# The last output block in row halves: the fifth product's share added by GpSimd, the first half's sum added to the last PSUM bank by TensorE, and that bank turned by VectorE straight from PSUM

## The chip, the cores and the metric

The kernel runs on one core of a Trainium2 chip. A core has five engines with a queue each: TensorE (PE, matmuls; PEld is its weight loads), VectorE (DVE), ScalarE (ACT), GpSimd (POOL) and SyncE (SP, which only issues transfers here). Each queue is worked off in order; engines wait for each other by semaphores. ScalarE issues some of the output transfers beside its own work. The metric is the device time of one execution in microseconds (us); lower is better.

## The reference

Pooled attention, then a feed-forward block with a snake activation:

```python
k_p = k.reshape(B, H, Sp, 8, D).mean(axis=3)        # B=8, H=8, S=576, D=64
v_p = v.reshape(B, H, Sp, 8, D).mean(axis=3)
attn = softmax(q @ k_p.T / sqrt(D)) @ v_p
x = attn.transpose(0, 2, 1, 3).reshape(4608, 512)
h = x @ w_in                                        # 512 -> 2048
g = h + sin(alpha * h) ** 2 / alpha
out = g @ w_out                                     # 2048 -> 512, float32
```

The change lies in the last matrix product, `g @ w_out`, and there in its last block alone.

## The kernel before

The first two thirds of the time are attention and `x @ w_in`; `g` goes through a buffer in HBM. The function `outputs` then computes `g @ w_out`, in eight units u of 576 rows (`self.B` units), by a two-level scheme of fast matrix multiplication with seven products instead of eight at each level. The outer seven products p run in the order `ORDER = (1, 2, 4, 6, 7, 5, 3)`; the loop over k takes the 56 pairs (u, n) one after the other, and a 57th pass finishes the last of them.

An outer product consists of seven inner products, `product(st, q, out, start)` (L1337), each a sum over `NJ` = 4 matmuls of 128x128 weights with 144 columns in fp32; the trace shows each such matmul as two records, eight for one inner product. The results are gathered in three PSUM banks: `x0` and `x1` with two parts of 144 columns each, and `yz`. The bank `x0` belongs to the first 144 rows of the half unit (i = 0), `x1` to the next 144 (i = 1). In both, part h = 0 and part h = 1 are two groups of 128 output columns. `yz[:, 1]`, the result of the fifth inner product, is a term z that both h = 1 parts still need. Pass k does products 1, 6 and 7 of its own outer product and, between them, 5, 4, 2 and 3 of the one before (functions `fifth`, `fourth`, `second`, `third`). ScalarE copies partial results from bank to bank (L1443, L1468, L1488).

When an outer product is complete, `combine` (L1370) adds its parts to block accumulators in SBUF, `c["a"]`, `c["b"]`, `c["c"]` (tiles `ca`, `cb`, `cc` of [128, 2, 2, 144], index h, then i). A finished block is turned in 32x32 squares by VectorE (`out`, L1357; L1362 is the transpose) into a tile `o`, and stored by four transfers (L1367). In the last unit the transfers alternate between the queues of SyncE and ScalarE (`both`).

The order of all instructions is the order in which the Python code emits them, engine by engine (`tc.manual_schedule`). Only the waits are put in by the framework.

The end of the kernel, with what the change touches:

- Pass 55 (p = 3 of the last unit starts): `combine` of p = 5 copies its banks to `cb`, adds z to it, lets GpSimd add all of `cb` to `cc` (L1390), lets VectorE add it to `ca`, and puts `ca`'s output on the list `later`, which runs at the end of this pass: one transpose and four transfers, two of them on ScalarE's queue.
- Pass 56, TensorE: products 5, 4, 2, 3 of the last p = 3, and nothing else.
- Pass 56, VectorE: after product 4, `early` (L1346) adds z to both h = 1 parts of `cc` and `x1` to its i = 1 half, and turns and stores the block's columns of rows 160 to 287 (`n0 = 5`: four groups of 32). After products 2 and 3, `combine` adds `x0` to the i = 0 half (L1412) and turns and stores rows 0 to 159.

Of the kernel before, what the change touches and what calls it, by code (L numbers as in the profile page):

```python
# [13 lines left out]
F32 = mybir.dt.float32  # L14
AX = mybir.AxisListType.X
AF = mybir.ActivationFunctionType
OP = mybir.AluOpType
PSUM = bass.MemoryType.PSUM

P = 128  # L20
# [20 lines left out]
class Kernel:  # L41
# [1248 lines left out]
    def outputs(self):  # L1290

        nc, T = self.nc, self.T
# [3 lines left out]
        add = lambda o, a, b: tt(o, a, b, OP.add)  # L1296
        X, C = {}, {}
        self.ne = False

        def outer(u, n):  # L1300
            r = self.R
            if n == 0:
                X[u] = {1: r["r11"], 2: r["r12"], 4: r["r22"]}
                return
            new = lambda p: self.gs.tile([P, self.NJ, JW, 2, T], F32, name=f"x{p}")[:]
            x = X[u]
            if n == 1:
                x[5] = new(5)
                tt(flat(x[5]), flat(r["r21"]), flat(x[4]), OP.add)
            if n == 2:  # L1310
                x[6] = new(6)
                tt(flat(x[6]), flat(x[5]), flat(x[1]), OP.subtract)
            if n == 3:
                x[7] = r["r21"]
                tt(flat(x[7]), flat(x[1]), flat(x[7]), OP.subtract)
            if n == 4:
                x[3] = new(3)
                tt(flat(x[3]), flat(x[2]), flat(x[6]), OP.subtract)
# [15 lines left out]
            yield  # L1334
            tt(s4, a(1, 2), s2, OP.subtract)

        def product(st, q, out, start):  # L1337
            A, W = st["A"][q], self.W[st["p"]][q]
            for J in range(self.NJ):
                nc.tensor.matmul(out, W[:, J // 2, J % 2, :], A[:, J, :], start=(start and J == 0), stop=(J == self.NJ - 1), skip_group_check=True)  # L1340

        def block(n):

            return self.op.tile([P, 2, 2, T], F32, name=n)

        def early(st):  # L1346

            t = C[st["u"]]["c"]
            with_z(t, st["yz"])
            add(t[:, :, 1], t[:, :, 1], st["x1"][:])  # L1350
            if st["u"] == self.B - 1:
                out(st["u"], 0, 1, t, 5, queues=both)

        def with_z(t, z):
            add(t[:, 1], t[:, 1], z[:, 1:2, :].to_broadcast([P, 2, T]))

        def out(u, i, j, t, n0=0, n1=2 * T // 32, queues=4 * (nc.sync,)):  # L1357

            if n0 or n1 * 32 == 2 * T:
                C[u]["o"] = self.op.tile([P, 2 * T // 32, 2, 32], F32, name="o", bufs=3)  # L1360
            o = C[u]["o"]
            nc.vector.transpose(out=o[:, n0:n1].rearrange("p n h c -> p h n c"),  # L1362
                                in_=t[:].rearrange("p h i c -> p h (i c)").rearrange("p h (n c) -> p h n c", c=32)[:, :, n0:n1])
            r = u * self.S + i * 2 * T
            for a in range(4):
                c = j * 2 * P + a * 64
                queues[a].dma_start(out=self.out[r + 32 * n0:r + 32 * n1, c:c + 64].rearrange("(n k) c -> k n c", k=32),  # L1367
                                        in_=o[32 * a:32 * a + 32, n0:n1].rearrange("k n h c -> k n (h c)"))

        def combine(st):  # L1370

            u, p, x, z = st["u"], st["p"], (st["x0"], st["x1"]), st["yz"]
            c = C.setdefault(u, {})

            def with_x(o, t):
                for i in range(2):
                    add(o[:, :, i], t[:, :, i], x[i][:])
            if p in (1, 4, 5):

                n = "a" if p == 1 else "b"  # L1380
                t = c[n] = block("c" + n)
                for i in range(2):
                    nc.scalar.copy(out=t[:, :, i], in_=x[i][:])
                with_z(t, z)
                if p == 5 and u < self.B - 1:
                    add(c["a"][:], c["a"][:], t[:])
                    out(u, 1, 1, c["a"])
                    add(c["c"][:], c["c"][:], t[:])
                elif p == 5:
                    nc.gpsimd.tensor_tensor(out=c["c"][:], in0=c["c"][:], in1=t[:], op=OP.add)  # L1390
                    add(c["a"][:], c["a"][:], t[:])
                    later.append(lambda: out(u, 1, 1, c["a"], queues=both))
            elif p == 2:
                o = block("cd")
                with_x(o, c["a"])
                with_z(o, z)
                out(u, 0, 0, o)
            elif p == 6:

                t = c["c"] = block("cc")  # L1400
                with_x(t, c["a"])
                with_z(t, z)
            elif p == 7:

                t = c["a"]
                with_x(t, c["c"])
                with_z(t, z)
                add(c["b"][:], c["b"][:], t[:])
                out(u, 1, 0, c["b"])
            else:  # L1410
                t = c["c"]
                add(t[:, :, 0], t[:, :, 0], x[0][:])  # L1412
                if u < self.B - 1:
                    out(u, 0, 1, t)
                else:
                    out(u, 0, 1, t, 0, 5, both)

        both = 2 * (nc.sync, nc.scalar)
        later = []
        last = None  # L1420
# [6 lines left out]
        for k in range(len(seq) + 1):  # L1427
            st = None
            if k < len(seq):
                u, n = seq[k]  # L1430
                st = {"u": u, "p": ORDER[n], "A": A.pop((u, n))}
                if 0 < n < 5 and k != 1:
                    outer(u, n)
                if n == 3 and u + 1 < self.B:
                    self.load_g(u + 1, ("r11", "r12", "r22"))
                if n == 5 and u + 1 < self.B:
                    self.load_g(u + 1, ("r21",))
                if n == 6 and u + 1 < self.B:
                    outer(u + 1, 0)
                x0 = st["x0"] = self.bank([P, 2, T])  # L1440
                yz = st["yz"] = self.abank([P, 2, T])
                product(st, 1, yz[:, 0, :], True)
                nc.scalar.copy(out=x0[:], in_=yz[:, 0:1, :].to_broadcast([P, 2, T]))  # L1443
                if k == 0:
                    yield
            def fifth():
                product(last, 5, last["yz"][:, 1, :], False)

            def fourth():
                product(last, 4, last["x1"][:, 0, :], False)  # L1450
                if last["p"] == 3:
                    early(last)

            def second():
                product(last, 2, last["x0"][:, 0, :], False)

            def third():
                product(last, 3, last["x0"][:, 1, :], False)

            if last:  # L1460
                fifth()
                if k == 1:
                    second()
                fourth()
            if st:
                product(st, 6, x0[:, 1, :], False)
                x1 = st["x1"] = self.bank([P, 2, T])
                nc.scalar.copy(out=x1[:, 0, :], in_=x0[:, 1, :])  # L1468
                if k + 1 < len(seq):
                    sums = inner(*seq[k + 1])  # L1470
                    next(sums)
                    if k == 0:
                        yield
                    next(sums)
            if last:
                if k != 1:
                    second()
                third()
                if k == 5:
                    self.inner_w(3, self.gs)  # L1480
                combine(last)
            for _ in sums:
                pass
            if k == 1:
                outer(0, 1)
            if st:
                product(st, 7, x1[:, 0, :], False)
                nc.scalar.copy(out=x1[:, 1, :], in_=x1[:, 0, :])  # L1488
            if later:
                later.pop()()  # L1490
            last = st
# [117 lines left out]
```

## Time and profile before

| | us |
|---|---|
| median of the runs (902.67, 902.79, 903.61) | 902.79 |
| the profiled execution, device time | 902.87 |
| its span, first to last instruction | 901.0 |
| TensorE busy (7010 matmul records) | 894.6 |
| VectorE busy | 678.0 |
| ScalarE busy | 447.9 |
| GpSimd busy | 212.5 |

Busy time overlaps between engines. The span begins with the first instruction; the device time has 1.87 us around it. Times in the text that look like 894.62 are microseconds from the span's start. A line such as `894.62 1.14 PE L1340 MATMUL ... x8` in the timeline gives start, duration of the whole group, engine, source line, operation, tiles (written<-read), shape and number; a matmul's record has 286 ns, but the next one starts 122.5 ns after it, since they are pipelined.

### The profile page before, as it was taken

To read this page: it belongs to the slowest core of one execution; us is meant where nothing else is said; L and a number is where in the kernel's file an instruction comes from. 1 tells how busy PE (TensorE), PEld (TensorE's weight loads), DVE (VectorE), ACT (ScalarE), POOL (GpSimd) and SP (SyncE) were. 2 spreads that over 40 slices of the span, in tenths; PEclk is the share of its full clock that TensorE was granted. 3 is DMA by queue.
4 is the path that set the end of the run, shared out by engine and by line. 5 is a ranking of instruction groups with operands and counts; after the bars stand their busy time and mean duration, and the time that the engine had idled before them with its cause. 6 is when DMAs were issued, how large, how long until landed. Compare 5 with 4: busy or idle time off the path is not lost.

```text
span 901.0 us, 17940 instructions
## 1 busy us (share of the span) xinstructions
PE 894.6 (99%) x7010; PEld 816.3 (91%) x7010; DVE 678.0 (75%) x1010; ACT 447.9 (50%) x1071; POOL 212.5 (24%) x218
## 2 busy tenths in 40 slices
PE   9999999999999999999999999999999999999998
PEld 5787888888888888888888999999999999999997
DVE  7776867768576675764558799979798888889895
ACT  5687776877768777687976611211111111111111
POOL 5698443825337262430000000000000000000000
PEclk9999999999999999999999999999999999999999
DMA  9957957759586585557226346261618172534401
GB/s 264 245 153 206 243 146 210 189 164 253 139 222 184 180 222 145 171 158 282 94 82 223 101 146 191 66 191 35 224 30 230 31 201 64 172 92 127 138 15 40
DMA packets 128371, 141.13 MB, mean 157 GB/s; under 512 B 46416, under 2 KB 95328, under 8 KB 128288
## 3 DMA queue, kind: packets, MB, share of 16 engines
q1 hardware_dynamic: 125504, 137.88, 53.4%
q10 hardware_dynamic: 2784, 2.11, 0.9%
q8 instruction: 56, 0.92, 0.5%
q14 instruction: 27, 0.22, 0.1%
HBM read 75.37 MB, written 47.19 MB: 136 GB/s over the span
## 4 chain that ended last, share of the span: by engine, by line
PE 97%; DVE 2%; DMA 1%; SPq 0%; issue 0%; ACT 0%; DVEq 0%
PE PS L848 46%; PE PS L1340 41%; PE PS L1038 3%; PE PS L317 2%; PE PS L612 2%; PE PS L625 1%; DMA h<-in_v_dram 1%; DVE x L1295 1%; DVE s L1295 0%; DVE r L1295 0%; PE PS L568 0%; PE PS L570 0%; PE PS L289 0%; PE PS L278 0%; PE PS L478 0%; SPq L164 0%
## 5 line engine op out<-in xcount | busy, mean ns | idle before, releaser
L848 PE MATMUL PS<-home,a 128*128 128x256 f32 x1104 | 258.1, 381 | 0.1
L848 PEld LDWEIGHTS PS<-home,a 128*128 128x128 f32 x1104 | 205.3, 190 | 32.3 <-issue 4.6
L848 PE MATMUL PS<-home,as 128*128 128x256 f32 x768 | 182.6, 381 | 0.0
L848 PEld LDWEIGHTS PS<-home,as 128*128 128x128 f32 x768 | 141.8, 190 | 19.7 <-ACT PS L822 1.2
L1390 POOL TENSOR_TENSOR cc<-cc,cb 128x576 f32<-128x576 f32 x1 | 2.0, 1977 | 501.7 <-DVE cb L1295 501.7
L1340 PE MATMUL PS<-s,wb 128*128 128x144 f32 x896 | 119.1, 286 | 0.0
L1340 PEld LDWEIGHTS PS<-s,wb 128*128 128x128 f32 x896 | 113.7, 190 | 0.1
L1015 ACT ACTIVATE s<-s,c 128x256 f32<-128x256 f32 (+1 forms) x228 | 113.5, 565 | 0.0
L821 DVE TENSOR_TENSOR h<-PS,p 128x512 f32<-128x512 f32 x72 | 49.3, 684 | 64.0 <-PE PS L848 37.4
L131 POOL TENSOR_TENSOR kvin<-kvin 96x768 f32<-96x768 f32 (+3 forms) x42 | 73.8, 1756 | 70.3 <-DMA kvin<-in_v_dram 68.1
L1468 ACT COPY PS<-PS 128x144 f32<-128x144 f32 x56 | 14.7, 263 | 145.0 <-PE PS L1340 138.4
L1008 ACT ACTIVATE s<-h,al 128x256 f32<-128x256 f32 x144 | 65.6, 509 | 38.3 <-DVE h L821 38.3
L1340 PE MATMUL PS<-r,wb 128*128 128x144 f32 x512 | 73.3, 286 | 0.3 <-DVE r L1295 0.3
L1340 PE MATMUL PS<-s,a 128*128 128x144 f32 x512 | 73.2, 286 | 0.0
L1008 ACT ACTIVATE s<-PS,al 128x256 f32<-128x256 f32 x144 | 60.2, 471 | 18.8 <-PE PS L848 17.9
L1060 DVE TENSOR_TENSOR h<-PS,s 128x512 f32<-128x512 f32 x36 | 24.8, 689 | 57.4 <-ACT s L1015 57.4
L1340 PEld LDWEIGHTS PS<-r,wb 128*128 128x128 f32 x512 | 67.1, 190 | 0.5 <-DVE r L1295 0.5
L1340 PEld LDWEIGHTS PS<-s,a 128*128 128x128 f32 x512 | 67.1, 190 | 0.0
L822 ACT COPY PS<-PS 128x512 f32<-128x512 f32 x72 | 41.5, 576 | 35.4 <-PE PS L848 30.6
L1488 ACT COPY PS<-PS 128x144 f32<-128x144 f32 x56 | 14.7, 263 | 88.1 <-PE PS L1340 88.1
L1340 PE MATMUL PS<-x,wb 128*128 128x144 f32 x384 | 54.9, 286 | 0.0
L1340 PE MATMUL PS<-s,we 128*128 128x144 f32 x384 | 54.9, 286 | 0.0
(216 smaller groups left out, 1407.5 us busy)
## 6 DMA issues: line engine op xcount, KB each, us to landing
g_bridge<-h SPq DMA_DIRECT2D x72, 512.0 KB
r<-g_bridge SPq DMA_DIRECT2D x31, 1152.0 KB
out_dram<-o SPq DMA_DIRECT2D x122, 72.0 KB
kvin<-in_k_dram SPq DMA_DIRECT2D x14, 576.0 KB
q<-in_q_dram SPq DMA_DIRECT2D x7, 1024.0 KB
kvin<-in_v_dram SPq DMA_DIRECT2D x14, 512.0 KB
aM<-tr SPq DMA_DIRECT2D x54, 92.0 KB
aM<-tr SPq DMA_DIRECT2D x54, 88.0 KB
```

What stands on the lines that cost most here:

```text
L131: self.nc.gpsimd.tensor_tensor(out=t[..., 0:w] if w > D else out, in0=t[..., 0:w], in1=t[..., w:2 * w], op=OP.add)
L317: nc.tensor.matmul(ps[e][r0 + r:r0 + r + q.shape[-1], h, :], q[s], kb[s, hp, :], start=True, stop=True)
L612: nc.tensor.matmul(o[r:r + 64], w, x, start=start and i < 2, stop=False, skip_group_check=True)
L821: add = lambda o, x, y: nc.vector.tensor_tensor(out=o, in0=x, in1=y, op=OP.add)
L822: copy = lambda o, x: nc.scalar.copy(out=o, in_=x)
L848: nc.tensor.matmul(ps[:, jj, :], self.A[p][:, kk, f * P:(f + 1) * P], x[:, kk, :], start=(start and n == 0), stop=(kk == 1), skip_group_ch ...
L1008: self.nc.scalar.activation(out=G.s[:, i, jj, j, :], in_=src[:, jj], func=AF.Sin, scale=self.al[:, f:f + 1])
L1015: self.nc.scalar.activation(out=x, in_=x, func=AF.Square, scale=self.c[:, f:f + 1])
L1038: nc.tensor.matmul(o, W[m][:, G.J - J0], X[m], start=start and n == 0, stop=True, skip_group_check=True)
L1060: add = lambda o, x, y: self.nc.vector.tensor_tensor(out=o, in0=x, in1=y, op=OP.add)
L1340: nc.tensor.matmul(out, W[:, J // 2, J % 2, :], A[:, J, :], start=(start and J == 0), stop=(J == self.NJ - 1), skip_group_check=True)
L1468: nc.scalar.copy(out=x1[:, 0, :], in_=x0[:, 1, :])
```

## The change

The last block (`cc` of unit 7 at p = 3) is handled in another way; all other blocks keep their instructions and order.

- GpSimd's one add of `cb` to `cc` becomes two, one for each row half i; the second of them is emitted in pass 56 (list `more`).
- z is no longer added by VectorE. ScalarE copies it from PSUM to a new tile `zc` (128x144), and GpSimd adds it to the h = 1 part of each half.
- `early` then adds `x1` to the i = 1 half as before. New: ScalarE copies 16 columns of that half (rows 144 to 159, h = 1) into the `x0` bank, behind its 288 columns, so that the bank holds rows 0 to 159 of h = 1 in one piece.
- In the third product, ahead of its last matmul, TensorE adds `cc[:, 1, 0]` to the bank by a matmul with the identity matrix.
- At the end VectorE adds `x0` only to the h = 0 part (128x144 instead of 128x288), turns 160 columns of that part from SBUF and 160 columns of the h = 1 part from the PSUM bank; the four transfers are as before.
- `out` is split into `turned` (the transpose) and `stored` (the transfers).

```diff
@@ -1334,9 +1334,11 @@
             yield
             tt(s4, a(1, 2), s2, OP.subtract)

-        def product(st, q, out, start):
+        def product(st, q, out, start, plus=None):
             A, W = st["A"][q], self.W[st["p"]][q]
             for J in range(self.NJ):
+                if plus is not None and J == self.NJ - 1:
+                    nc.tensor.matmul(out, self.ident[:], plus, start=False, stop=False, skip_group_check=True)
                 nc.tensor.matmul(out, W[:, J // 2, J % 2, :], A[:, J, :], start=(start and J == 0), stop=(J == self.NJ - 1), skip_group_check=True)

         def block(n):
@@ -1345,27 +1347,42 @@

         def early(st):

-            t = C[st["u"]]["c"]
-            with_z(t, st["yz"])
+            t, z = C[st["u"]]["c"], st["yz"]
+            if st["u"] < self.B - 1:
+                with_z(t, z)
+                add(t[:, :, 1], t[:, :, 1], st["x1"][:])
+                return
             add(t[:, :, 1], t[:, :, 1], st["x1"][:])
-            if st["u"] == self.B - 1:
-                out(st["u"], 0, 1, t, 5, queues=both)
+            nc.scalar.copy(out=self.PS[:, st["bank"]][:, 2 * T:2 * T + 16], in_=t[:, 1, 1, 0:16])
+            o = C[st["u"]]["o"] = self.op.tile([P, 2 * T // 32, 2, 32], F32, name="o", bufs=3)
+            turned(o, row(t), 5, 9)
+            stored(st["u"], 0, 1, o, 5, 9, both)

         def with_z(t, z):
             add(t[:, 1], t[:, 1], z[:, 1:2, :].to_broadcast([P, 2, T]))

-        def out(u, i, j, t, n0=0, n1=2 * T // 32, queues=4 * (nc.sync,)):
-
-            if n0 or n1 * 32 == 2 * T:
-                C[u]["o"] = self.op.tile([P, 2 * T // 32, 2, 32], F32, name="o", bufs=3)
-            o = C[u]["o"]
-            nc.vector.transpose(out=o[:, n0:n1].rearrange("p n h c -> p h n c"),
-                                in_=t[:].rearrange("p h i c -> p h (i c)").rearrange("p h (n c) -> p h n c", c=32)[:, :, n0:n1])
+        def row(t):
+
+            return t[:].rearrange("p h i c -> p h (i c)")
+
+        def turned(o, t, n0, n1, h0=0, h1=2):
+
+            nc.vector.transpose(out=o[:, n0:n1, h0:h1].rearrange("p n h c -> p h n c"),
+                                in_=t[:, h0:h1, 32 * n0:32 * n1].rearrange("p h (n c) -> p h n c", c=32))
+
+        def stored(u, i, j, o, n0, n1, queues=4 * (nc.sync,)):
+
             r = u * self.S + i * 2 * T
             for a in range(4):
                 c = j * 2 * P + a * 64
                 queues[a].dma_start(out=self.out[r + 32 * n0:r + 32 * n1, c:c + 64].rearrange("(n k) c -> k n c", k=32),
                                         in_=o[32 * a:32 * a + 32, n0:n1].rearrange("k n h c -> k n (h c)"))
+
+        def out(u, i, j, t, queues=4 * (nc.sync,)):
+
+            o = self.op.tile([P, 2 * T // 32, 2, 32], F32, name="o", bufs=3)
+            turned(o, row(t), 0, 9)
+            stored(u, i, j, o, 0, 9, queues)

         def combine(st):

@@ -1387,7 +1404,9 @@
                     out(u, 1, 1, c["a"])
                     add(c["c"][:], c["c"][:], t[:])
                 elif p == 5:
-                    nc.gpsimd.tensor_tensor(out=c["c"][:], in0=c["c"][:], in1=t[:], op=OP.add)
+                    for i in (1, 0):
+                        more.append((c["c"][:, :, i], t[:, :, i]))
+                    plus(*more[0])
                     add(c["a"][:], c["a"][:], t[:])
                     later.append(lambda: out(u, 1, 1, c["a"], queues=both))
             elif p == 2:
@@ -1409,12 +1428,21 @@
                 out(u, 1, 0, c["b"])
             else:
                 t = c["c"]
-                add(t[:, :, 0], t[:, :, 0], x[0][:])
                 if u < self.B - 1:
+                    add(t[:, :, 0], t[:, :, 0], x[0][:])
                     out(u, 0, 1, t)
-                else:
-                    out(u, 0, 1, t, 0, 5, both)
-
+                    return
+                o = c["o"]
+                add(t[:, 0, 0], t[:, 0, 0], x[0][:, 0])
+                turned(o, row(t), 0, 5, 0, 1)
+                nc.vector.transpose(out=o[:, 0:5, 1], in_=self.PS[:, st["bank"]][:, T:T + 160].rearrange("p (n c) -> p n c", c=32))
+                stored(u, 0, 1, o, 0, 5, both)
+
+        def plus(o, x):
+
+            nc.gpsimd.tensor_tensor(out=o, in0=o, in1=x, op=OP.add)
+
+        more = []
         both = 2 * (nc.sync, nc.scalar)
         later = []
         last = None
@@ -1438,6 +1466,7 @@
                 if n == 6 and u + 1 < self.B:
                     outer(u + 1, 0)
                 x0 = st["x0"] = self.bank([P, 2, T])
+                st["bank"] = self.turn
                 yz = st["yz"] = self.abank([P, 2, T])
                 product(st, 1, yz[:, 0, :], True)
                 nc.scalar.copy(out=x0[:], in_=yz[:, 0:1, :].to_broadcast([P, 2, T]))
@@ -1449,13 +1478,20 @@
             def fourth():
                 product(last, 4, last["x1"][:, 0, :], False)
                 if last["p"] == 3:
+                    if last["u"] == self.B - 1:
+                        t, zc = C[last["u"]]["c"], self.op.tile([P, T], F32, name="zc", bufs=1)
+                        nc.scalar.copy(out=zc[:], in_=last["yz"][:, 1, :])
+                        plus(t[:, 1, 1], zc[:])
+                        plus(*more[1])
+                        plus(t[:, 1, 0], zc[:])
                     early(last)

             def second():
                 product(last, 2, last["x0"][:, 0, :], False)

             def third():
-                product(last, 3, last["x0"][:, 1, :], False)
+                at_end = last["u"] == self.B - 1 and last["p"] == 3
+                product(last, 3, last["x0"][:, 1, :], False, C[last["u"]]["c"][:, 1, 0] if at_end else None)

             if last:
                 fifth()
```

## The prediction

> **What bounds the kernel now.** I read the chain that ended last first, because the edit touches only the last block of the last unit. Its shares over the whole span:
>
> ```profile
> PE 97%; DVE 2%; DMA 1%; SPq 0%; issue 0%; ACT 0%; DVEq 0%
> ```
>
> TensorE sets the time; VectorE and the transfers count only where TensorE has run out. The same chain for the stretch from 880 us:
>
> ```profile
> 879.96 16.80 PE PS L1340 x137
> 896.75 0.02 issue
> 896.77 0.47 DVE cc L1295
> 897.24 0.02 issue
> 897.26 0.51 DVE o L1362
> ```
>
> So the end is: TensorE without a gap to 896.74 us, one VectorE add, one transpose to 897.77, then the last output transfer and the closing of the program, 3.27 us up to 901.04. The last stretch, engine by engine, from the timeline (start, duration, what; the bracket is idle time and who ended it):
>
> ```profile
> 893.14 1.98 POOL L1390 TENSOR_TENSOR cc<-cc,cb 128x576 f32<-128x576 f32 x1 [501.68 <-DVE cb L1295]
> 893.63 1.14 PE L1340 MATMUL PS<-x,we 128*128 128x144 f32 x8
> 893.89 0.78 DVE L1362 STREAM_TRANSPOSE o<-ca 128x576 f32<-128x576 f32 x1
> ...
> 894.62 1.14 PE L1340 MATMUL PS<-x,wb 128*128 128x144 f32 x8
> ...
> 894.70 3.97 ACTq L1367 DMA_DIRECT2D out_dram<-o  x6
> 895.15 1.04 DVE L1295 TENSOR_TENSOR cc<-cc,PS 128x288 f32<-128x288 f32 x2 [0.49 <-POOL cc L1390]
> ...
> 895.60 1.14 PE L1340 MATMUL PS<-s,wb 128*128 128x144 f32 x8
> 896.23 0.45 DVE L1362 STREAM_TRANSPOSE o<-cc 128x256 f32<-128x256 f32 x1
> 896.77 0.46 DVE L1295 TENSOR_TENSOR cc<-cc,PS 128x288 f32<-128x288 f32 x1
> 897.26 0.51 DVE L1362 STREAM_TRANSPOSE o<-cc 128x320 f32<-128x320 f32 x1
> ```
>
> To be seen: the fourth product (from 893.63), the second (from 894.62) and the third (from 895.60) follow each other at 122.5 ns a matmul; nothing holds TensorE. GpSimd's one add ends at 895.12, VectorE waits 0.49 us for it, and that wait is covered by TensorE, which runs to 896.74. ScalarE's queue holds the six output issues behind VectorE's transposes; the first two are the store of `ca`:
>
> ```profile
> 894.70 0.89 ACTq L1367 DMA_DIRECT2D out_dram<-o  x2
> 895.12 0.47 ACTq L1367 DMA_DIRECT2D out_dram<-o  x1
> ```
>
> They wait for the transpose that ends at 894.67 and keep the queue until 895.59. That matters after the change: ScalarE starts no later instruction while it issues. Elsewhere in this trace:
>
> ```profile
> 66.65 2.81 ACTq L523 DMA_DIRECT2D aM<-tr  x4
> 69.51 0.91 ACT L1008 ACTIVATE s<-h,al 128x256 f32<-128x256 f32 x2 [3.81 <-DVE h L821]
> ```
>
> The activation begins 0.05 us after the fourth issue ends (66.65 + 2.81 = 69.46); the engine stood idle during all four.
>
> **The change, part by part.** Up to `ca`'s transpose (894.67) and its two issues (895.59), every engine has the same instructions in the same order, so these times stay. From there the built program has a new chain through five engines. Its waits: `zc` stands on ScalarE behind the two issues of `ca`; GpSimd's second add waits for `zc`; VectorE's early add (`cc[:, :, 1] += x1`) for that add; ScalarE's 16-column copy into the last bank for the early add; and the first matmul of the *second product* for that copy, although it writes columns 0 to 143 of the bank and the copy columns 288 to 303 (same bank, earlier in program order). Before, the second product waited for nothing. Queued behind it on TensorE is all that is left: second product, third product, identity matmul; VectorE's last add waits for their end, and the last transfers for VectorE.
>
> Step by step, with durations from rows:
>
> - `zc`, 128x144 from PSUM: 895.59 + 0.05 = 895.64. The 128x128 copy from PSUM at L384 has 271 ns, the 128x288 one at L1383 402: 0.28, end 895.92. Bounds: at 514.92 an issue of 0.39 us let the next activation start 0.25 us after its beginning, so 0.14 to 0.18 us earlier; not later.
> - GpSimd, 128x144 add of `zc`: its first add (the `i=1` half of t) starts at 893.14 as before. GpSimd adds of 64, 128 and 256 columns take 321, 457 and 727 ns (L131), about 0.19 us + 2.1 ns a column. For 288 that is 0.80, plus at most the 0.58 us by which the 128x576 add exceeded this line (1.98 against 1.40): end by 894.52, hidden under ScalarE's issues. The `zc` add starts 0.08 us after its releaser (893.06 to 893.14), 896.00, and takes 0.49: end 896.49. The upper bound is the 946 ns of the slow 128x128 row at L806, +0.46; VectorE waits during this add, so I take the undisturbed rows.
> - VectorE's early add, 128x288 with PSUM: 0.03 + 0.455: 896.52 to 896.98.
> - ScalarE's copy of 128x16, SBUF to PSUM: no such row. Below is the 128x1 copy at L619 (160 ns), above the 128x64 one at L392 (213); 0.18. With 0.03 for the release, end 897.19.
> - TensorE: a released weight load starts 0.05 us after its releaser (535.78 to 535.83), 897.24 instead of 894.62: **a stall of 2.62 us**. In that same row the second matmul came 0.227 us after the first, not 0.122: +0.11. Then 16 matmuls as before and two more for the identity (one fp32 matmul is two records): +0.245. Last end 896.74 + 2.62 + 0.11 + 0.245 = 899.71.
> - Identity matmul's own wait: GpSimd goes on from 896.49 with 0.07 + 0.80 and 0.07 + 0.49 to 897.92; TensorE comes to it at 897.24 + 0.1 + 14 x 0.1225 = 899.06. Cost nothing, covered by the second and third products; if TensorE did not stall, they would reach it at 896.33 and that cover would be gone.
> - VectorE's end: the 128x288 add (0.455) becomes 128x144, on the line of L1295's PSUM adds and L821's (288: 0.455, 512: 0.684, so 1.02 ns a column) 0.31. The 128x320 transpose (0.511) becomes two of 128x160: 256 and 320 columns took 0.445 and 0.511, so 0.345 each, the second from PSUM. No row has a transpose out of PSUM; bounds 0.168 (128x32 from SBUF, L513) and 0.511 (twice the size), taken 0.345, since a 512-column add with a PSUM operand (L821, 684 ns) costs no more than one without (L742, 684). Sum with gaps 0.04 + 0.31 + 0.03 + 0.345 + 0.03 + 0.345 = 1.10 us, against 1.04 before (896.74 to 897.775): +0.06.
> - The early half's store leaves at about 897.5 instead of 896.7 and is issued by 898.4, 2.4 us ahead of the last store; hidden. The last store is the same four transfers of 40 KB, and the 3.27 us tail stays; with nothing beside it, it could gain some 0.2.
>
> Sum: 2.62 + 0.11 + 0.245 + 0.06 = **+3.03 us**, last transpose at 900.81, span 904.07. The profiled execution took 902.87 (span 901.0 and 1.87 around it), so 905.90; that execution lies 0.08 above the median of 902.79, so I forecast **905.8 us**. Own bounds: -0.8 (0.18 earlier `zc`, 0.18 cheaper PSUM transpose, 0.1 overlap of the transposes, 0.1 restart, 0.2 tail, rounded) and +0.7 (0.46 GpSimd, 0.17 transpose, 0.05 copy).
>
> [...]
>
> **The rivals.**
>
> *The clock drops in the stall.* The windows of the profile show clock, DMA share and rate last:
>
> ```profile
> 892.00:896.80 4.80, 4.74 (x39) 4.52 (x37) 3.37 (x7) 0.84 (x3) 1.98 (x1) 1.00 0.26 54
> 896.80:899.00 2.20, 0.00 (x0) 0.00 (x0) 0.94 (x2) 0.00 (x0) 0.00 (x0) 1.00 0.53 114
> 899.00:900.30 1.30, 0.00 (x0) 0.00 (x0) 0.00 (x0) 0.00 (x0) 0.00 (x0) 1.00 0.36 74
> 900.30:901.00 0.70, 0.00 (x0) 0.00 (x0) 0.00 (x0) 0.00 (x0) 0.00 (x0) 0.52 0.00 0
> ```
>
> After the last matmul (896.74) the grant stays 1.00 to 900.30 and then halves, 3.6 us later. A stall of 2.5 us from the last matmul's end is shorter. If it halved all the same, 18 matmuls would take 0.12 us more each: +2.2, 908.0. The longest start-to-start gap of TensorE in the trace is 1.0 us, so nothing shows a stall this long. [...]
>
> *`zc` does not queue behind `ca`'s store* (the side of no change). Place: ScalarE's queue at 893.8, where the fifth product is done. Price: `zc` is then ready at 894.1, GpSimd's first add (894.52) decides, its `zc` add ends 895.08 instead of 896.49, everything after moves 1.4 us forward: +1.63, 904.4, which is within 0.2%. It decides from a `zc` start 1.2 us earlier than forecast, before 894.4. Against it: the order on the queue, and 69.46 to 69.51 above. The issues could only be passed if ScalarE's DMA instructions did not wait in line.
>
> *The second product is not held* (its wait was already met). TensorE then comes to the identity matmul at 896.33 and waits for GpSimd's last add, 897.92, to restart at 897.97; four matmuls end at 898.7, VectorE at 899.8: +2.0, 904.9. The wait stands in the built program on a count that only the copy reaches, so this is unlikely.
>
> *It gains.* With no wait at all TensorE has 0.245 more and VectorE 0.06 more: +0.3. To end earlier, both transposes would have to cost under 0.2 us each, below the 0.202 of a 128x64 one (L509). I see no path to it; a few hundredths for what I overlook.
>
> **Chances.** Forecast mechanism 0.81 (905.0 to 906.6); clock 0.04 (908.0); no queueing 0.05 (904.4); second product not held 0.05 (904.9); no cost or gain 0.05 (903.1 and below). What a measurement tells from no change is about 0.2%, 1.8 us. Faster by more: 0.02; slower by more: the forecast, the clock and the free second product, less a little for spread of the medians (runs of before differ by 0.94), 0.89; the rest, 0.09, same. The range takes the mechanism's bounds and the 904.9 case, plus some spread: 904.7 to 906.8.
>
> **What would show it.** Right: an idle stretch of TensorE of some 2.4 to 2.7 us ahead of the second product, ended by the ScalarE copy; `zc` starting right behind two issues at about 895.6; GpSimd's four adds ending at about 897.9 without TensorE waiting for them; last transpose ending near 900.8; no change before 894.6. Wrong: `zc` before 895, a second product that starts at 894.6, a clock below 1.00 before 899.7, or a PSUM transpose far from 0.345.

## The result and the profile after

Over six runs each, the changed kernel takes 907.08 us (906.06 to 908.15), the kernel before 902.89 (902.27 to 903.61): ratio 1.0044, interval 1.0034 to 1.0054. It is slower by 4.2 us where 3.0 were forecast (905.8 against 902.79), and 907.08 lies 0.3 us above the range. The profiled execution took 908.15, the slowest of the six.

The page of the changed kernel: span, and the chain that ended last by engine.

```profile
span 905.7 us, 17950 instructions
PE 96%; DVE 2%; DMA 1%; SPq 0%; ACT 0%; issue 0%; ACTq 0%; POOL 0%; DVEq 0%; POOLq 0%
```

TensorE's share has fallen by a point, and ScalarE's queue (ACTq), GpSimd (POOL) and GpSimd's queue (POOLq) have entered the chain. The same chain for the end alone, in order of time (start, duration, what):

```profile
893.68 0.79 DVE o L1370
...
894.49 0.38 ACTq L1378
...
894.91 0.47 ACTq L1378
...
895.42 0.29 ACT zc L1483
...
895.84 0.50 POOL cc L1443
...
896.36 0.46 DVE cc L1295
...
896.85 0.18 ACT PS L1356
897.03 0.04 issue
897.07 3.65 PE PS L1342 x14
900.73 0.24 PE PS L1341 x2
900.97 0.26 PE PS L1342 x2
```

This is the chain forecast from the built program, link by link: `ca`'s transpose, two issues on ScalarE's queue, `zc`, GpSimd, VectorE, the 16-column copy, and only then TensorE's second product. Before, TensorE stood at the head of this stretch by itself. The last three lines hold what was not in the sum: 14 matmul records take 3.65 us, 0.26 each, then four take 0.50, 0.125 each. TensorE's rows in the timeline, and the windows (after the busy times: granted clock, DMA share, GB/s):

```profile
893.42 1.14 PE L1342 MATMUL PS<-x,we 128*128 128x144 f32 x8
...
897.07 2.26 PE L1342 MATMUL PS<-x,wb 128*128 128x144 f32 x8 [2.50 <-ACT PS L1356]
...
899.13 1.60 PE L1342 MATMUL PS<-s,wb 128*128 128x144 f32 x6
...
900.81 0.41 PE L1342 MATMUL PS<-s,wb 128*128 128x144 f32 x2
```

```profile
894.50:897.00 2.50, 0.07 (x1) 0.00 (x0) 0.61 (x2) 0.43 (x2) 1.16 (x2) 1.00 0.58 118
897.00:900.00 3.00, 2.93 (x12) 2.93 (x13) 0.29 (x1) 0.02 (x1) 0.57 (x2) 0.52 0.21 44
```

Eight matmul records of the same shape take 2.26 us behind the stall and 1.14 ahead of it, and the mean grant in the window that begins at 897.00 is 0.52. The trace's clock record has the grant at one half from 897.135 to 900.548.

Runs begin their body up to 0.7 us earlier or later against the span's start, so I compare executions below by one stretch that starts with the block itself: from the start of the fourth product (`x,we`) to the end of the last transpose. Before: 893.635 to 897.775, **4.14 us**. Changed: 893.425 to 902.269, **8.84 us**, 4.70 more.

### The profile page after: what moved, and what is told of

Same layout as the page of the kernel before. It is cut to its first block, busy times and chain, and to the rows that moved or that the text cites. A ratio compares the mean times of both kernels' runs of the same rounds, so it can differ in the third digit from the quotient of the medians.

```text
span 905.7 us, 17950 instructions
## 1 busy us (share of the span) xinstructions
PE 896.7 (99%) x7012; PEld 818.6 (90%) x7012; DVE 679.3 (75%) x1010; ACT 448.0 (49%) x1073; POOL 213.4 (24%) x221
## 4 chain that ended last, share of the span: by engine, by line
PE 96%; DVE 2%; DMA 1%; SPq 0%; ACT 0%; issue 0%; ACTq 0%; POOL 0%; DVEq 0%; POOLq 0%
PE PS L848 45%; PE PS L1342 41%; PE PS L1038 3%; PE PS L317 2%; PE PS L612 2%; PE PS L625 1%; DMA h<-in_v_dram 1%; DVE x L1295 1%; DVE s L1295 0%; DVE r L1295 0%; PE PS L568 0%; PE PS L570 0%; PE PS L289 0%; PE PS L278 0%; PE PS L478 0%; SPq L164 0%
## 5 line engine op out<-in xcount | busy, mean ns | idle before, releaser
L1443 POOL TENSOR_TENSOR cc<-cc,cb 128x288 f32<-128x288 f32 x2 | 2.2, 1083 | 501.8 <-DVE cb L1295 501.8
```

## The experiments

Two questions: is the loss the chain of waits, link by link as forecast, and is the rest the clock?

**again.** The changed kernel, no edit.

> The changed kernel once more, as the yardstick for the other three on the same chip. In its profile the second product is held for 2.5 us, and then 14 of its last 18 matmul records come 0.24 us apart instead of 0.1225, in a window in which the granted clock is one half; its six runs spread from 906.06 to 908.15 us, before over 1.3 us. Theory A (the halving of the clock falls into the stall at a place that differs from run to run, and takes between nothing and 2.1 us): a median near 907.1, a spread of over 1.5 us again, and in another profile the same chain of waits to within 0.1 us up to the second product, but the edge of the half clock at another place. Rival B (the surplus over the forecast is fixed, for instance a slower restart of TensorE after every stall): the slow matmuls stand at the same place again and the spread is that of before.

906.19 us (905.98 to 908.53) against 902.64, ratio 1.0045 (1.0032 to 1.0059). The median is 0.9 us below the 907.1 expected. In its profile the stretch is 8.85 us and the stall 2.51, as in the first profile of the changed kernel to 0.01. The half clock begins at 896.769, that is 0.20 us behind the restart at 896.57, and lasts 3.413 us again (mean grant 0.95, 0.50 and 0.94 in 894.5:897, 897:900 and 900:901.5); 14 records of the second and third products and the first of the identity matmul's are 0.24 apart. So the edge moves against the restart, but only by 0.14 us in these two profiles. The spread of the times (2.6 us) does not tell A from B: the kernel before spread over 3.3 us in its 13 runs here.

**warm.** Work for TensorE in the stall, into an unused bank.

```diff
+                if not st:
+                    for _ in range(11):
+                        nc.tensor.matmul(self.psum([P, 4, P], (self.turn + 1) % 5), self.full[:], self.full[:].unsqueeze(1).to_broadcast([P, 4, P]), start=True, stop=True)
                 if k != 1:
                     second()
```

> Eleven bf16 matmuls of 512 columns into a bank that nobody reads, put between the fourth and the second product: about 2.3 us of TensorE work in a stall of 2.5 us, so the second product should start when it did, at about 897.1 us. They change nothing that is stored. Theory A (the clock): granted clock 1.00 until after the last matmul in every run, 0.1225 us between the records, last matmul at about 899.5, span 903.6 to 904.0, median 906.0 to 906.3, spread below 1 us. Rival B (the surplus is not the clock): 907.1 as the changed kernel, or more, with records still 0.24 us apart.

906.71 us (906.26 to 906.91). The clock half of theory A came in, the time did not. Timeline and window of `warm`:

```profile
894.26 1.58 ACTq L1378 DMA_DIRECT2D out_dram<-o  x2
...
897.53 1.25 PE L1342 MATMUL PS<-x,wb 128*128 128x144 f32 x8 [0.82 <-ACT PS L1356]
```

```profile
897.00:900.00 3.00, 2.47 (x18) 2.26 (x18) 0.72 (x2) 0.18 (x1) 1.03 (x2) 1.00 0.26 53
```

The clock stays 1.00 and the second product takes 1.25 us instead of 2.26. But the two issues in front of `zc` took 1.58 us instead of 0.89, and everything behind them is later by the difference. The stretch is 7.86 us: 0.69 longer by the issues, 1.67 shorter by the clock. The median alone would have misled.

**again2 and warm_two.** The changed kernel once more, and the stall filled with two matmuls in place of eleven.

> The changed kernel as yardstick on this chip, and one more look at where the half clock begins. So far it began 0.06 and 0.20 us after the second product restarted (897.14 for 897.07, 896.77 for 896.57), each time at a whole number of windows of 3.413 us after the clock first rose to 1.00. Theory A (the grid of windows lies differently in each run; a window that is mostly the stall halves the clock for the next): again whole windows from the first rise, a median of 906 to 907.5, spread over 1.5 us.

> The stall filled again, but with two fp32 identity matmuls of 512 columns (about 0.86 us each) in place of eleven bf16 ones, since with the eleven the second output issue on ScalarE took 1.16 us instead of 0.47, and so held zc. TensorE is then idle for some 0.7 us of the stall. Theory A (clock): no half clock before the last matmul, second product to last transpose in 3.5 us instead of 5.2; with issues of 0.4 to 0.5 us a span near 903.7 and a median of 905.6 to 906.2 with a spread below 1 us. Rival E (what the eleven matmuls changed was something else, and the clock halves here too): 5.2 us from second product to last transpose.

```diff
+                if not st:
+                    for _ in range(2):
+                        nc.tensor.matmul(self.psum([P, 4 * P], (self.turn + 1) % 5), self.ident[:], row(C[u]["b"])[:, :, 0:256], start=True, stop=True)
                 if k != 1:
                     second()
```

`again2`: 907.42 us (906.95 to 908.31, a spread of 1.4 where over 1.5 was expected), ratio 1.0054 (1.0041 to 1.0066); stretch 8.85 us, half clock from 897.540, 0.19 behind the restart at 897.35 (mean grant 1.00, 0.59 and 0.68 in 894.5:897, 897:900 and 900:901.5, so 3.4 us of it). `warm_two`: 906.8 us (906.12 to 907.45), ratio 1.0044 (1.0032 to 1.0057). Its timeline:

```profile
894.34 1.14 PE L1342 MATMUL PS<-x,we 128*128 128x144 f32 x8
...
895.32 1.88 PE L1514 MATMUL PS<-cb,ident 128*128 128x512 f32 x4
895.40 0.90 ACTq L1378 DMA_DIRECT2D out_dram<-o  x2
...
898.00 1.25 PE L1342 MATMUL PS<-x,wb 128*128 128x144 f32 x8 [0.80 <-ACT PS L1356]
...
901.22 0.31 DVE L1438 STREAM_TRANSPOSE o<-PS 128x160 f32<-128x160 f32 x1
```

Now the issues take 0.90 us, the second product starts 3.66 us behind the fourth as in the changed kernel (3.65), and the only difference is the clock: from its start to the last transpose 3.52 us instead of 5.20. The stretch is 894.34 to 901.52 = 7.18 us, 3.04 above before; the forecast had 3.03 for exactly these terms. So in these profiles the chain was priced right, and the missing 1.67 us are the clock. The median did not follow: it is 0.6 us above the expected range and only 0.6 below `again2`. In the two profiled executions 0.65 us of the gain are taken back because the body of `warm_two` began that much later; and not every run of the changed kernel lost the 1.67 us (next section).

**sp_store.** One link of the chain undone: ScalarE has no issue in front of `zc`.

```diff
-                    later.append(lambda: out(u, 1, 1, c["a"], queues=both))
+                    later.append(lambda: out(u, 1, 1, c["a"]))
```

> The changed kernel, but the four transfers of ca are all issued by SyncE, so that zc on ScalarE has no DMA issue in front of it. Theory A (ScalarE's two issues hold zc): zc starts at about 893.9 as soon as the fifth product is done, GpSimd's first add (ending 894.3 to 894.5) decides next, the second product starts near 895.7 instead of 897.1, and with a stall of about 1.2 us in a window of 3.4 the clock stays at 1.00: median near 904.8, that is 1.9 above before, with a spread below 1 us. Rival C (the chain is bound elsewhere, by GpSimd or the early add): within 0.3 us of the changed kernel.

904.60 us, ratio 1.0021 (1.0011 to 1.0030), 2.0 above before where 1.9 were expected, with a spread of 1.5 where below 1 was expected. Timeline:

```profile
893.66 0.28 ACT L1483 COPY zc<-PS 128x144 f32<-128x144 f32 x1 [0.72 <-PE PS L1342]
...
894.42 0.49 POOL L1443 TENSOR_TENSOR cc<-cc,zc 128x144 f32<-128x144 f32 x1
...
895.66 1.25 PE L1342 MATMUL PS<-x,wb 128*128 128x144 f32 x8 [1.05 <-ACT PS L1356]
```

`zc` goes as soon as the fifth product is done, GpSimd's first add decides next, and the stall shrinks from 2.50 to 1.05 us. With it the half clock is gone from the products (1.25 us for the second where the changed kernel has 2.26; mean granted clock of the profiled run 1.000 where that has 0.997): stretch 5.72 us, 1.58 above before. That the median came out near the 1.9 is in part luck: in this profile 0.53 us more lie behind the last transpose, where two store issues took 2.66 us (last section). Theory A holds, C falls. The queue in front of `zc` cost 1.45 us by itself and 1.67 by the clock.

**copy_late.** The copy into the bank emitted behind the third product.

```diff
-            nc.scalar.copy(out=self.PS[:, st["bank"]][:, 2 * T:2 * T + 16], in_=t[:, 1, 1, 0:16])
...
                 o = c["o"]
+                nc.scalar.copy(out=self.PS[:, st["bank"]][:, 2 * T:2 * T + 16], in_=t[:, 1, 1, 0:16])
                 add(t[:, 0, 0], t[:, 0, 0], x[0][:, 0])
```

> The changed kernel, but the copy of 16 columns into the last bank is emitted after the third product, so nothing but the identity matmul can hold TensorE. Theory A (the second product is held by that copy, through the bank, and by nothing else): second product at 894.4 to 894.6 without a gap, the third up to its last matmul, then TensorE waits at the identity matmul for GpSimd's last add, to about 897.7; last matmul ends near 898.4, the copy hides beside VectorE's add, last transpose ends near 899.6: median 905.0 to 905.5, with at most four matmuls at half clock. Rival D (the second product is held by something else too): TensorE idle before the second product as in the changed kernel and 907 us.

905.86 us, ratio 1.0035 (1.0022 to 1.0047), 0.4 above the expected range. Timeline:

```profile
894.65 1.14 PE L1342 MATMUL PS<-x,wb 128*128 128x144 f32 x8
...
898.29 0.51 PE L1341 MATMUL PS<-cc,ident 128*128 128x144 f32 x2 [1.76 <-POOL cc L1443]
```

No gap ahead of the second product, and TensorE waits at the identity matmul for GpSimd's last add instead. So the copy was the one thing that held the second product (D falls), and undoing it alone only shows the next wait, as the forecast had it for that rival. Of what is over, 0.34 us are the issues in front of `zc`, which took 1.23 us here instead of 0.89; and the copy did not hide, VectorE's add waited for it (the next run shows the line).

**sp_late.** Both edits together.

> The changed kernel with both holds undone: the store of ca on SyncE alone, and the copy of 16 columns after the third product. Theory A (the holds and the clock are the whole loss; the identity matmul and the rest of the new arithmetic cost little): zc at 893.7, GpSimd's last add done near 896.2, TensorE without a stall or with one below 0.2 us at the identity matmul, last matmul near 896.9 to 897.1, then copy, add and two transposes in 1.25 us: 0.3 to 0.6 us above before, 902.9 to 903.3 on a chip where before has 902.64; not to be told from before. Rival F (the new arithmetic itself costs): more than 1.8 us above before.

903.58 us against 902.80, ratio 1.0009 (1.0000 to 1.0018): not to be told from before, at most a little slower. Stretch 4.87 us, 0.73 above before; that and the 0.78 between the medians are a little over the 0.3 to 0.6 expected. TensorE is held for 0.14 us at the identity matmul and does 0.245 more, and behind it comes the copy, which now stands before VectorE's add:

```profile
896.93 0.17 ACT L1435 COPY PS<-cc 128x16 f32<-128x16 f32 x1 [3.20 <-PE PS L1342]
897.21 0.30 DVE L1295 TENSOR_TENSOR cc<-cc,PS 128x144 f32<-128x144 f32 x1 [1.54 <-ACT PS L1435]
```

The new arithmetic costs little (F falls) and gains nothing: what VectorE does behind the last matmul is 1.05 us in the changed kernel and was 1.04 before.

**by_columns.** Is it the bank that holds, or the columns? The kernel before, with the last half turned by column groups.

```diff
...
+        def half(st, h):
+            t = C[st["u"]]["c"]
+            add(t[:, h, 0], t[:, h, 0], st["x0"][:, h])
+            turn(C[st["u"]]["o"], t, 0, 5, h, h + 1)
...
                 product(last, 2, last["x0"][:, 0, :], False)
+                if not st:
+                    half(last, 0)
```

> The kernel before, with its last half turned by column groups: VectorE adds and turns the h = 0 part as soon as the second product is done, and the h = 1 part after the third. The add reads columns 0 to 143 of the bank while the third product has to write columns 144 to 287. Theory A (the program orders accesses by bank, so a reader or writer of other columns holds the next product): third product held from 895.6 until VectorE's add ends, about 897.0; after it only a 128x144 add and a 128x160 transpose, 0.35 us less than before: last transpose near 898.9, 1.0 to 1.3 us above before. Rival G (different columns do not hold): third product at 895.6, last transpose near 897.4, 0.3 us below before.

904.07 us, ratio 1.0013 (1.0004 to 1.0022). Stretch 5.25 us, 1.11 above before, inside A's 1.0 to 1.3. TensorE's third product in the timeline:

```profile
895.97 0.27 DVE L1295 TENSOR_TENSOR cc<-cc,PS 128x144 f32<-128x144 f32 x1
...
896.29 1.25 PE L1340 MATMUL PS<-s,wb 128*128 128x144 f32 x8 [1.16 <-DVE cc L1295]
```

It writes columns 144 to 287 and waits 1.16 us for a reader of columns 0 to 143. So this program orders accesses by bank, not by columns.

**hold_short and hold_long.** The stall without the change: the kernel before, with a copy into unused columns of the last bank, and in `hold_long` four more copies ahead of it.

```diff
                 x0 = st["x0"] = self.bank([P, 2, T])
+                st["bank"] = self.turn
...
                 if last["p"] == 3:
+                    if not st:
+                        scratch = self.op.tile([P, P], F32, name="scratch", bufs=1)
+                        for _ in range(4):
+                            nc.scalar.copy(out=scratch[:], in_=self.ident[:])
+                        nc.scalar.copy(out=self.PS[:, last["bank"]][:, 2 * T:2 * T + 16], in_=self.ident[:, 0:16])
                     early(last)
```

> The kernel before with nothing of the change but a hold: ScalarE copies 16 columns of the identity into columns 288 to 303 of the last bank, behind the two issues of ca and ahead of the second product; nobody reads them. Theory A: the second product is held until about 895.87 (stall 1.25 us), clock 1.00 to the end of the products; from the fourth product's start to the last transpose 4.14 + 1.25 + 0.1 = 5.5 us; median 1.3 to 1.5 above before. If columns that nobody else uses do not hold (rival G): 4.14 us and the time of before.

> The same, with four 128x128 copies of the identity into a scratch tile on ScalarE ahead of the 16 columns, so that the second product is held until about 897.0 (stall 2.4 us, as in the changed kernel). Theory A (a stall of this length halves the clock for part of the products, one of 1.25 does not): from the fourth product's start to the last transpose 4.14 + 2.4 + 0.1 = 6.65 us without the half clock and up to 8.5 with it; a half clock from an edge in or behind the stall, at a whole number of 3.413 us from the first rise; median 2.6 to 4.6 above before, spread wider than in hold_short. Rival H (in the changed kernel it was the new arithmetic, not the stall, that slowed the matmuls): 6.65 us with 0.1225 us between all records.

`hold_short` 904.35 us, ratio 1.0017 (1.0008 to 1.0026), 1.6 above before where at most 1.5 were expected, stretch 5.56 us; `hold_long` 907.00 us (905.48 to 908.14), ratio 1.0041 (1.0027 to 1.0055), stretch 8.42 us. The second product in each, and the window that holds it in `hold_long`:

```profile
895.46 1.25 PE L1340 MATMUL PS<-x,wb 128*128 128x144 f32 x8 [1.08 <-ACT PS L1454]
```

```profile
896.52 2.17 PE L1340 MATMUL PS<-x,wb 128*128 128x144 f32 x8 [2.27 <-ACT PS L1457]
```

```profile
896.70:900.20 3.50, 3.50 (x16) 3.50 (x16) 0.00 (x0) 0.00 (x0) 0.00 (x0) 0.52 0.21 42
```

1.19 us more of stall make the stretch 2.86 us longer; the rest, 1.67, is the half clock (from 896.678; mean grant 0.52 in the window above, 1.00 in the ones before and behind it). H falls: without any of the new arithmetic, a stall of this length does the same. The stall of 1.1 us in `hold_short` costs little beyond itself: the second product starts 1.24 us later against the fourth, and the stretch is 1.42 longer.

## Why the prediction was wrong

What was right, with the numbers of the profiled execution. `zc` began 0.04 us behind the second issue (forecast 0.05) and took 0.28 (0.28); GpSimd's `zc` add 0.49 (0.49), the early add 0.45 (0.455), the 16-column copy 0.175 (0.18). The second product started 3.65 us behind the fourth, where before it was 0.98: a stall of 2.67 (2.62). Restart and identity, from the second product's start to the last matmul's end, cost 0.35 (0.355), read in `warm_two` where the clock does not hide it (2.47 against 2.12). VectorE's end is 1.05 us (1.10): the transpose out of PSUM took 0.31 (0.345) and began 0.08 us before the one ahead of it ended. GpSimd did not hold the identity matmul. That the sum of the stretch came out to 0.01 us (3.04 in `warm_two` for 3.03) is in part luck: the stall was 0.06 longer and VectorE's end 0.05 shorter than forecast. The two halves of GpSimd's add differ: the same 128x288 add takes 1.37 us beside `ca<-ca,cb`, which has two SBUF inputs, and 0.80 later, beside the early add (0.45, one input in PSUM) and the first 0.23 us of a transpose; no run isolates what makes the difference. The lines of the changed kernel:

```profile
892.89 0.76 DVE L1295 TENSOR_TENSOR ca<-ca,cb 128x576 f32<-128x576 f32 x1
892.93 1.37 POOL L1443 TENSOR_TENSOR cc<-cc,cb 128x288 f32<-128x288 f32 x1 [501.80 <-DVE cb L1295]
...
896.28 0.80 POOL L1443 TENSOR_TENSOR cc<-cc,cb 128x288 f32<-128x288 f32 x1
```

**What failed is the rival "The clock drops in the stall".** Its price was near (+2.2 forecast, 1.67 measured in each of the four profiles that show it), its chance of 0.04 was not. The step was: "After the last matmul (896.74) the grant stays 1.00 to 900.30 and then halves, 3.6 us later. A stall of 2.5 us from the last matmul's end is shorter." The 3.6 us were read as the idle time that it takes. They are not: in the changed kernel the grant halved 0.06 us behind the restart, after 2.50 us without a matmul, and at the end 2.7 us behind TensorE's last matmul. The changed kernel's clock record has 1.0 from 6.256, 0.5 from 897.135, 1.0 from 900.548 and 0.5 from 903.961: first 890.879 us, which is 261 times 3.4133, then twice 3.413. The record of the kernel before has 1.0 from 6.029 and 0.5 from 900.321, 894.292 us or 262 times 3.4133 later. Counted in such intervals, the 3.6 us of the kernel before are the 0.17 us that were left of one and the whole next one, in which no matmul ran. The share of an interval of 3.413 us in which a matmul record runs, worked out from the matmul records of the profiles, and the clock in the interval behind it:

| profile | busy share of the interval | clock behind it |
|---|---|---|
| before, interval behind TensorE's end | 0.00 | 0.5 |
| changed, interval that holds TensorE's end | 0.20 | 0.5 |
| changed, again, again2 (stall 2.5 us) | 0.27, 0.26, 0.26 | 0.5 |
| hold_long (stall 2.3 us) | 0.34 | 0.5 |
| hold_short, last products | 0.65 | 1.0 |
| before, last products | 0.95 | 1.0 |

In these profiles the half clock follows shares of up to 0.34 and the full clock those of 0.65 and 0.95; what lies between is not shown. My estimate from the 3.413 us: a stall of 2.5 us can by itself leave an interval 0.27 busy (1 - 2.5 / 3.413), one of 1.1 us no less than 0.68. Where the intervals lie against the block differs: the fourth product starts 887.17 us behind the record's first 1.0 in the changed kernel and 887.61 before. So I estimate the loss at between nothing and some 2 us (18 records, 0.12 us more each). The mean granted clock that every run lists fits that: 3.413 us at half clock in a span of 904 us brings the mean to 0.998. Seven of the sixteen runs of the changed kernel (`again` and `again2` with them) have 0.999 or 1.000 and spans of 903.5 to 904.5, mean 904.0, where the forecast had 904.07; the other nine have 0.996 to 0.998 and spans of 904.7 to 906.3, mean 905.4. All three profiles fell among the nine, with the edge 0.06 to 0.20 us behind the restart each time; no profile shows a stall of this length without the half clock.

**A second term failed beside it, the "1.87 around it" that the forecast carried over from the kernel before without a reason.** The time outside the span is 2.4 to 2.5 us in all six runs of the result and 2.2 to 2.5 in all sixteen, against less than 2.0 in all 49 runs of the kernel before that were taken beside the experiments. The median needed both to leave the range: the median span, 904.6, with the old 1.87 would have been 906.5, and so would the forecast span with the new 2.45. Why this time grew stays open (last section).

For the profiled execution, the slowest of the six, the whole can be added up. From 902.87 to 908.15 it is: stall +2.67, TensorE +2.02 (0.35 forecast, 1.67 clock), VectorE +0.01, tail from the last transpose to the end +0.18, body of the run 0.21 earlier, and time outside the span +0.61 (2.44 instead of 1.83). Without the clock and this last term the sum is 905.87, the forecast.

The rivals of the queue and of the second product can be held against experiments: `sp_store` came to +1.58 in the stretch (forecast +1.63), and `copy_late` to +2.52 (+2.0), of which 0.34 are the longer issues and some 0.25 the copy ahead of VectorE's add, which that rival did not have.

## What to carry to other kernels

Read a new dependency from the built program, link by link, with every queue that a link passes: two output issues ahead of a small copy cost 1.45 us here, and a copy into unused columns of a bank held the product that followed. If TensorE is to wait, keep the wait near a microsecond, or give it something to do: at 1.05 and 1.08 us (`sp_store`, `hold_short`) the products kept the full clock, at 2.3 to 2.5 us the wait was followed by another 1.7 us of loss at half clock in all four profiles, though by the mean clock not in every run. And compare profiles by a stretch that belongs to the block; the medians here move by half a microsecond for reasons outside it.

## What the hardware showed that was not expected

Output issues took longer beside an instruction fetch. The instruction queue of the trace fetches mostly 16 KB at a time (55 packets with 0.90 MB in the changed kernel, 27 with 0.22 MB beside them). In three profiles an output issue that followed another one directly, while such a fetch was under way or began within 0.15 us, ended 0.40 to 0.45 us behind the fetch: `warm` (fetch to 895.41, issues to 895.83), `copy_late` (895.51, 895.96), `sp_store` (898.16, 898.56; that issue and the one ahead of it took 2.66 us, the same two 0.79 in the changed kernel). Where no fetch ran, as in the changed kernel, the second issue took 0.47. A fetch does not always cost: in `before` (fetch to 895.15) the second issue also took 0.47. That is a coincidence in time seen several times; nothing was changed to test it.

The time outside the span was 1.83 us in `before`, whose trace has no fetch behind the last instruction up to 904, 2.44 in the changed kernel, whose trace has two there (16 KB at 906.1, 8 KB at 907.9), and 2.93 in `hold_short`, which has one (16 KB at 904.3). The other profiled executions had 1.86 to 1.91 (`sp_store`, `copy_late`, `sp_late`, `by_columns`) and 2.2 to 2.4 (`again`, `again2`, `warm`, `warm_two`, `hold_long`). What decides when the fetch comes stays open.
